# Projections written feature-major in 512-wide matmuls, transposes by DMA, weight gradients in 288 to 432 wide tiles

## The chip, the cores and the metric

One core of a Trainium2 chip runs the whole program, forward and backward. The metric is the device time of one execution in microseconds. The kernel before takes 5262.92 us (median of 3 runs, 5261.9 to 5267.33).

## The reference

The layer mixes two branches for one sequence of S = 2048 tokens of D = 576 features, and the kernel returns its output and all gradients for a given grad_out:

```
q, k, v = split(x @ wqkv)                    # H = 32 heads of 18
p = softmax(q k^T * 18^-0.5);  a = (p v) @ wo
b = fft_convolution(u, K(A, B, C, dt)) + u * Dskip   # S4, N = 128 states, u = x
g = sigmoid(sum(x * gate_w))
out = g * a + (1 - g) * b
gradients of x, wqkv, wo, A, B, C, log_dt, Dskip, gate_w
```

## The kernel before

The program has four stages, one behind the other. Tensors go between them through DRAM, and each has its own SBUF and PSUM pools, so that a stage can only load what fits after the pools of the stage before are given up. Within stage 1, post and S4 a scheduler orders each engine's instructions; in attention the order on PE, ACT, DVE and POOL is written out by hand, and the scheduler orders only the DMA queue. Every DMA here, transposes too, is issued by SP, in order, with at most eight outstanding.

**Stage 1 (lines 96 to 248).** x is loaded token-major and turned into xT (features on partitions) by 80 PE transposes of 128 x 128, each with a copy out of PSUM by DVE or ACT (lines 117 to 121); wo likewise by 25 (line 129). Then for K, Q and V in turn, for each of 16 token tiles and each of 11 chunks of 3 heads (54 columns), five matmuls accumulate over the 576 features (`ps_proj`, two PSUM buffers), and ACT (line 168) or DVE (line 170) copies the chunk into `Xa`, in which each head has 32 columns (18 and padding), with column 18 as an additional row for the softmax shift: 1 for K and V, and for Q minus the product of the norms, from squares, sums and the largest key norm (lines 178 to 187). `Xa` is stored token-major (line 191) and turned by 384 PE transposes (line 198) with copies (lines 200 and 202) into feature-major tiles of 4 heads x 32 rows, 2048 tokens wide, stored per group of heads as `QaT_d`, `KaT_d`, `VaT_d` (line 204). The gate is one more column of the last V chunk. Then grad_out times the gate (`d_a`, line 223) is transposed by 80 PE transposes, and dO = d_a wo^T is made in 960 matmuls of 48 columns (line 241) and stored at once at the end (line 248).

**Attention (lines 260 to 533).** Eight groups of four heads, four blocks of 512 queries each, forward and backward interleaved by hand. `load_group` loads a group's QaT, KaT, VaT (line 282) and the token-major Vtok, Ktok, Qtok (line 285); Ktok and Qtok have one buffer. A step makes scores twice (19 rows of contraction, 512 wide), takes two exponentials on ACT (lines 510 and 514), multiplies into `ds` on DVE (line 519), and each `ds` tile is transposed by a DMA (line 525); `accO`, `accV`, `accQ` and `accK` collect the products.

**Post (lines 536 to 678).** A first pool: O is loaded, transposed by 80 PE transposes, multiplied by wo in 960 matmuls of 48 columns (`ps_a`), reduced against grad_out for the gate's gradient (lines 577 and 578), stored times the gate; and wo's gradient in 960 matmuls of 48 (`ps_dwo`). A second pool: x and the gradient of qkv (`dqkv`) are loaded (lines 616 and 618), wqkv's gradient is made in 2880 matmuls of 48 columns, sixteen token tiles accumulated in each (`ps_dwq`), wqkv and dqkv are transposed on PE (70 and 224), and dx is made in 2688 matmuls of 48 (`ps_dx`) and stored.

**S4 (from line 702)** computes the convolution branch, its gradients and the outputs.

Of the kernel before, what the change touches and what calls it, by code (L numbers as in the profile page):

```python
# [9 lines left out]
A = mybir.AluOpType  # L10
ACT = mybir.ActivationFunctionType
BF = mybir.dt.bfloat16
# [5 lines left out]
P = 128  # L18


def build(tc, aps, dbg_aps=None, stages=("s1", "attn", "post", "s4", "final")):
# [39 lines left out]
    with ExitStack() as gctx:  # L61
# [19 lines left out]
        Qtok_d = dram.tile([P, NT * H * HP], BF, name="Qtok_d")  # L81
        Ktok_d = dram.tile([P, NT * H * HP], BF, name="Ktok_d")
        Vtok_d = dram.tile([P, NT * H * HP], BF, name="Vtok_d")
# [5 lines left out]

        with ExitStack() as ctx:  # L90
            s1 = ctx.enter_context(tc.tile_pool(name="s1", bufs=1))
            work = ctx.enter_context(tc.tile_pool(name="s1work", bufs=2))
            psA = ctx.enter_context(tc.tile_pool(name="s1psA", bufs=2, space=bass.MemoryType.PSUM))
            psB = ctx.enter_context(tc.tile_pool(name="s1psB", bufs=2, space=bass.MemoryType.PSUM))

            x_tok = s1.tile([P, NT, D], BF, name="x_tok")
            nc.sync.dma_start(x_tok, x2.rearrange("(t p) d -> p t d", p=P))
            wqkv_sb = s1.tile([P, DC, F + 1], BF, name="wqkv_sb")
            gate_w2 = gate_w.rearrange("(d o) -> d o", o=1)
            for c, (d0, dsz) in enumerate(dch):  # L100
                if dsz < P:
                    nc.gpsimd.memset(wqkv_sb[dsz:P, c, :], 0.0)
                nc.sync.dma_start(wqkv_sb[0:dsz, c, 0:F], wqkv[d0:d0 + dsz, :])
                nc.sync.dma_start(wqkv_sb[0:dsz, c, F:F + 1], gate_w2[d0:d0 + dsz, :])
            wo_sb = s1.tile([P, DC, D], BF, name="wo_sb")
            for c, (f0, fsz) in enumerate(dch):
                if fsz < P:
                    nc.gpsimd.memset(wo_sb[fsz:P, c, :], 0.0)
                nc.sync.dma_start(wo_sb[0:fsz, c, :], wo[f0:f0 + fsz, :])
            xT = s1.tile([P, DC, S], BF, name="xT")  # L110
            cnt = 0
            for c, (d0, dsz) in enumerate(dch):
                if dsz < P:
                    nc.vector.memset(xT[dsz:P, c, :], 0.0)
                for t in range(NT):
                    pt = psB.tile([P, P], BF, tag="tp", name="pt_x")
                    nc.tensor.transpose(pt[0:dsz, :], x_tok[:, t, d0:d0 + dsz], ident_bf)
                    if cnt % 2 == 0:
                        nc.vector.tensor_copy(xT[0:dsz, c, t * P:(t + 1) * P], pt[0:dsz, :])
                    else:  # L120
                        nc.scalar.copy(xT[0:dsz, c, t * P:(t + 1) * P], pt[0:dsz, :])
                    cnt += 1
            woT_sb = s1.tile([P, DC, D], BF, name="woT_sb")
            for c, (e0, esz) in enumerate(dch):
                if esz < P:
                    nc.vector.memset(woT_sb[esz:P, c, :], 0.0)
                for fc_, (f0, fsz) in enumerate(dch):
                    pt = psB.tile([P, P], BF, tag="tp", name="pt_w")
                    nc.tensor.transpose(pt[0:esz, 0:fsz], wo_sb[0:fsz, fc_, e0:e0 + esz], ident_bf[0:fsz, 0:fsz])
                    if cnt % 2 == 0:  # L130
                        nc.vector.tensor_copy(woT_sb[0:esz, c, f0:f0 + fsz], pt[0:esz, 0:fsz])
                    else:
                        nc.scalar.copy(woT_sb[0:esz, c, f0:f0 + fsz], pt[0:esz, 0:fsz])
                    cnt += 1

            sg = s1.tile([P, NT], F32, name="sg")
            qsq = s1.tile([P, NT, H], F32, name="qsq")
            kmx2 = s1.tile([P, H], F32, name="kmx2")
            mt = s1.tile([P, NT, H], F32, name="mt")
            hchunks = []  # L140
            h0 = 0
            while h0 < H:
                nh = min(3, H - h0)
                hchunks.append((h0, nh))
                h0 += nh
            MAXW = 3 * DH + 1
            cnt = 0
            for which in (1, 0, 2):
                Xa = s1.tile([P, NT, H, HP], BF, tag="Xa", name="Xa")
                (nc.gpsimd if which != 0 else nc.vector).memset(Xa, 0.0)  # L150
                if which != 0:
                    nc.vector.memset(Xa[:, :, :, DH], 1.0)
                scl = c_scale if which == 0 else 1.0
                for t in range(NT):
                    for hi, (h0, nh) in enumerate(hchunks):
                        f0 = which * D + h0 * DH
                        fsz = nh * DH
                        last = (which == 2 and hi == len(hchunks) - 1)
                        if last:
                            fsz += 1  # L160
                        ps = psA.tile([P, MAXW], F32, tag="proj", name="ps_proj")
                        for c, (d0, dsz) in enumerate(dch):
                            mm(ps[:, 0:fsz], lhsT=xT[:, c, t * P:(t + 1) * P], rhs=wqkv_sb[:, c, f0:f0 + fsz],
                               start=(c == 0), stop=(c == DC - 1))
# [1102 lines left out]
```

## Time and profile before

| | us |
|---|---|
| median of 3 runs | 5262.92 (5261.9 to 5267.33) |
| the profiled execution | 5259.65 |
| its span | 5257.9 |
| PE busy in the span | 3442.0 (65%) |
| DVE busy | 3203.6 (61%) |
| ACT busy | 3065.4 (58%) |
| POOL busy | 551.4 (10%) |

The span runs from the first to the last recorded instruction. In the views below a group's row has the line, the engine, the operation, output <- input, partitions x elements and the number of instructions; behind the bar stand their busy time, the mean of one in ns, and the idle time of the engine just before them with what ended most of it. A window's row has busy time and count for each engine, then the granted TensorE clock (1.00 is full), the DMA engines' busy share and GB/s. A timeline's row has its start, its duration, and the idle time before it in brackets.

### The profile page before, as it was taken

What the parts mean: (1) busy time and instruction counts of PE and PEld (TensorE: products, weight loads), DVE (VectorE), ACT (ScalarE), POOL (GpSimd) and SP (SyncE); (2) the same over time, 40 slices, a digit from 0 to 9 for tenths busy, and PEclk for the clock granted to TensorE, in tenths of its full rate; (3) what the DMA queues carried; (4) which work ended last, traced back from release to release, by engine and by line L of the source; (5) the groups of instructions that cost most, each with busy time, mean ns of one, the idle gap of its engine ahead of it and who ended that gap; (6) DMA issues with size and microseconds to landing.
All of it is one profiled execution on the core that took longest, in us unless ns stands there. A gap on an engine that the chain in (4) does not pass through costs nothing. (4 is left out here: it accounts for less than half of the span.)

```text
span 5257.9 us, 87333 instructions
## 1 busy us (share of the span) xinstructions
PE 3442.0 (65%) x34473; PEld 1477.7 (28%) x34473; DVE 3203.6 (61%) x6274; ACT 3065.4 (58%) x6102; POOL 551.4 (10%) x750
## 2 busy tenths in 40 slices
PE   7678999999999999999999698022222222222221
PEld 5453222222222222222222586011112222211210
DVE  4433777777777777767777433200176677776668
ACT  4336998989898998989896323000053343444321
POOL 1000000000000000000000000300023333333330
PEclk8555555555555555555555788555555555555555
DMA  2123667776767767776767401322345445444436
GB/s 97 73 77 81 122 122 137 124 133 124 136 120 131 128 123 134 125 134 120 126 122 137 162 25 59 98 65 58 97 116 122 114 110 124 101 113 122 120 89 167
DMA packets 1683053, 589.85 MB, mean 112 GB/s; under 512 B 1606222, under 2 KB 1654544, under 8 KB 1672658
## 3 DMA queue, kind: packets, MB, share of 16 engines
q1 hardware_dynamic: 1682642, 584.27, 52.6%
q8 instruction: 270, 4.42, 0.3%
q14 instruction: 141, 1.16, 0.1%
HBM read 205.89 MB, written 72.07 MB: 53 GB/s over the span
## 5 line engine op out<-in xcount | busy, mean ns | idle before, releaser
L519 DVE TENSOR_TENSOR ds<-ps_P,PT 128x512 bf16<-128x512 f32 x2048 | 1328.6, 686 | 470.1 <-PE ps_P L30 262.0
L510 ACT ACTIVATE PT<-ps_P 128x512 bf16<-128x512 f32 x2048 | 1226.5, 603 | 154.5 <-PE ps_P L30 102.6
L514 ACT ACTIVATE eb<-ps_P 128x512 bf16<-128x512 f32 x2048 | 1236.0, 605 | 19.8 <-PE ps_P L30 19.3
L30 PE MATMUL ps_P<-dOaT,VaT_g 19*128 19x512 bf16 x2048 | 1197.4, 601 | 29.6 <-DMA VaT_g<-VaT_d 28.5
L30 PE MATMUL ps_P<-KaT_g,QaT_g 19*128 19x512 bf16 x2048 | 1164.7, 593 | 7.6 <-ACT PT L510 7.6
L30 PE MATMUL ps_P<-QaT_g,KaT_g 19*128 19x512 bf16 x2048 | 1053.9, 615 | 14.8 <-DMA KaT_g<-KaT_d 12.3
L30 PE MATMUL uvr<-RX,E1e 128*128 128x64 bf16 x576 | 72.4, 290 | 648.3 <-DVE E1e L932 648.3
L30 PE MATMUL accO<-PT,Vtok_g 128*32 128x512 bf16 x2048 | 331.1, 631 | 1.1 <-DMA Vtok_g<-Vtok_d 1.1
L30 PEld LDWEIGHTS <-KaT_g 19*128 19x128 bf16 x2048 | 135.7, 103 | 694.9 <-issue 669.0
L30 PEld LDWEIGHTS <-E1e 128*128 128x128 bf16 x1152 | 119.7, 123 | 724.8 <-DVE E1e L932 629.8
L30 PEld LDWEIGHTS <-VaT_g 19*128 19x128 bf16 x2048 | 197.4, 98 | 437.0 <-issue 404.8
L30 PE MATMUL accK<-dsT,Qtok_g 128*32 128x256 bf16 x4096 | 314.7, 406 | 1.8 <-DVE dqa L396 1.0
L878 ACT COPY mst<-psM 128x512 f32<-128x512 f32 x36 | 21.9, 609 | 441.1 <-PE psM L30 368.8
L30 PE MATMUL accQ<-ds,Ktok_g 128*32 128x512 bf16 x2048 | 266.9, 620 | 1.2 <-DVE dvacc L379 1.2
L30 PE MATMUL accV<-eb,dOa 128*32 128x512 bf16 x2048 | 266.9, 620 | 0.6 <-DVE dkacc L420 0.6
L546 POOL MEMSET wo_sb<- 64x576 bf16 x1 | 0.6, 573 | 2429.9 <-DMA dqkv_d<-dtk 2429.9
L865 DVE TENSOR_SCALAR xs<-xs,msk 128x3072 bf16<-128x3072 bf16 x21 | 21.4, 1020 | 379.1 <-DMA xs<-in_A_x_dram 379.1
L30 PE MATMUL psM<-xs,gyp 128*32 128x128 bf16 x576 | 54.7, 550 | 263.2 <-DMA xs<-in_A_x_dram 133.8
L30 PE MATMUL ybp<-Rw,E1n 128*128 128x31 bf16 x1152 | 71.4, 233 | 225.7 <-POOL Rw L1013 220.4
L924 ACT ACT_TABLE_LOAD x35 | 44.9, 1283 | 291.8 <-DMA abuf<-ath_d 291.6
L30 PE MATMUL ps_proj<-wqkv_sb,xT 128*128 128x54 bf16 (+2 forms) x2640 | 171.9, 218 | 43.0 <-ACT Xa L168 31.0
L30 PEld LDWEIGHTS <-QaT_g 19*128 19x128 bf16 x2048 | 178.8, 100 | 51.3 <-issue 27.6
(332 smaller groups left out, 5525.1 us busy)
## 6 DMA issues: line engine op xcount, KB each, us to landing
abuf<-ath_d SPq DMA_DIRECT2D x36, 1024.0 KB
thb<-ath_d SPq DMA_DIRECT2D x36, 1024.0 KB
T0w<-Kp_d SPq DMA_DIRECT2D x36, 512.0 KB
dsT<-ds SPq DMA_TRANSPOSE x512
dqkv_d<-dtk SPq DMA_DIRECT2D x96, 72.0 KB
dqkv_tok<-dqkv_d SPq DMA_DIRECT2D x1, 6912.0 KB
Md_d<-mst SPq DMA_DIRECT2D x144, 36.0 KB
x_tok<-in_A_x_dram SPq DMA_DIRECT2D x2, 2304.0 KB
```

Of the source, the lines that this page charges most:

```text
L30: return nc.tensor.matmul(out, lhsT=lhsT, rhs=rhs, start=start, stop=stop, **kw)
L510: nc.scalar.activation(U["PT"][i][:, j, :], ps, ACT.Exp)
L514: nc.scalar.activation(e, ps, ACT.Exp)
L519: nc.vector.tensor_tensor(U["ds"][i][:, j, :], ps, U["PT"][i][:, j, :], op=A.mult)
L546: nc.gpsimd.memset(wo_sb[fsz:P, c, :], 0.0)
L865: nc.vector.tensor_scalar(xs[:, dl, :, :], xs[:, dl, :, :], msk[:, dl:dl + 1], None, op0=A.mult)
L878: nc.scalar.copy(mst[:, :, 0:P], psM)
L924: nc.scalar.activation(abuf, abuf, ACT.Exp, scale=l0col)
```

## The change

Stage 1 loads x with its feature dimension padded to 640 and makes xT by four DMA transposes. wqkv is copied into `Wp`, where each head's 18 columns are padded with zeros to 32, so that a matmul with 128 columns of `Wp` as weights and 512 tokens of xT as the moving operand writes four heads feature-major into PSUM, in the layout that the old transposes made: 480 matmuls of 512, three PSUM buffers. The eviction adds the constant row (`onec`) or scales; for K and Q a square, and a matmul with a 0/1 matrix `hsel` that sums each head's squares into its row 18, give the norms. Tiles are ordered by group of heads, and K, Q, V within it. wo and d_a are transposed by DMA too, and dO is made in 160 matmuls of 288 with one PSUM buffer of two banks, stored per token tile.

On PE the new order in stage 1 around the end of a group's Q (`ps_proj_778` is the last Q tile, `sq_785` and `ps2_787` its squares and their sums, `ps_proj_794` and `801` are V):

```order
L30 MATMUL ps_proj_794<-xT_97,Wp_124 128x512
L30 LDWEIGHTS hsel_137
L30 MATMUL ps2_773<-sq_771,hsel_137 128x512
L30 LDWEIGHTS Wp_124
L30 MATMUL ps_proj_794<-xT_97,Wp_124 128x512
L30 LDWEIGHTS Wp_124
L30 MATMUL ps_proj_794<-xT_97,Wp_124 128x512
L30 LDWEIGHTS hsel_137
L30 MATMUL ps2_787<-sq_785,hsel_137 128x512
L30 LDWEIGHTS Wp_124
L30 MATMUL ps_proj_794<-xT_97,Wp_124 128x512
```

A head-sum matmul stands four to seven projections behind the last one of its own tile, and PE takes its instructions in this order. Before, PE ran five projections of a chunk and then the next chunk's.

In attention, `load_group` makes Vtok, Ktok and Qtok by DMA transposes from the feature-major stores; the token-major stores are gone. On SP at the end of a group, before:

```order
L282 DMA QaT_g<-QaT_d 128x2048
L282 DMA VaT_g<-VaT_d 128x2048
L525 DMA_TRANSPOSE dsT<-ds 128x16x128
L282 DMA KaT_g<-KaT_d 128x2048
L341 DMA dqkv_d<-dtk 128x4x72
L285 DMA Ktok_g<-Ktok_d 128x16x128
L525 DMA_TRANSPOSE dsT<-ds 128x16x128
L341 DMA dqkv_d<-dtk 128x4x72
```

and now:

```order
L241 DMA QaT_g<-QaT_d 128x2048
L241 DMA VaT_g<-VaT_d 128x2048
L484 DMA_TRANSPOSE dsT<-ds 128x16x128
L241 DMA KaT_g<-KaT_d 128x2048
L300 DMA dqkv_d<-dtk 128x4x72
L244 DMA_TRANSPOSE Ktok_g<-KaT_d 128x16x128
L484 DMA_TRANSPOSE dsT<-ds 128x16x128
L300 DMA dqkv_d<-dtk 128x4x72
```

The places in the queue are the same; the plain loads have become transposes. On ACT and DVE the order in attention is the same.

Post has one pool. All its inputs are issued at once, wqkv's gradient comes first (320 matmuls of 432 columns, sixteen token tiles accumulated in each), then the output projection (160 of 288, O transposed by four DMA transposes, the gate's gradient by one fused instruction per tile), dx (448 of 288, dqkv transposed by sixteen DMA transposes, three buffers), and most of wo's gradient (160 of 288) last. On SP behind attention, now:

```order
L500 DMA O_tok<-O_d 128x16x576
L503 DMA wo_sb_37550<-in_A_wo_dram 128x576 x4
L503 DMA wo_sb_37550<-in_A_wo_dram 64x576
L505 DMA x_tok_b<-in_A_x_dram 128x16x576
L508 DMA dqkv_tok<-dqkv_d 128x16x1728
L512 DMA wq_pad<-in_A_wqkv_dram 128x1728 x4
L512 DMA wq_pad<-in_A_wqkv_dram 64x1728
L515 DMA_TRANSPOSE wqkvT<-wq_pad 128x14x128 x5
L537 DMA_TRANSPOSE OT_37945<-O_tok 128x20x128
```

Before, x and dqkv stood behind all of the output projection's stores. In S4 only a row sum is merged from 12 matmuls into 2.

The diff, cut to its core (of what is removed, the section on the kernel before tells):

```diff
@@ stage 1: start, weights, gate, d_a
-            psA = ctx.enter_context(tc.tile_pool(name="s1psA", bufs=2, space=bass.MemoryType.PSUM))
+            psA = ctx.enter_context(tc.tile_pool(name="s1psA", bufs=3, space=bass.MemoryType.PSUM))
...
+            for tb in range(NBK):
+                nc.sync.dma_start(x_pad[:, tb * TB:(tb + 1) * TB, 0:D], x_v0[:, tb * TB:(tb + 1) * TB, :])
             for c, (d0, dsz) in enumerate(dch):
+                nc.sync.dma_start(wqkv_sb[0:dsz, c, :], wqkv[d0:d0 + dsz, :])
+                nc.sync.dma_start(gw_sb[0:dsz, c:c + 1], gate_w2[d0:d0 + dsz, :])
+            for tb in range(NBK):
+                nc.sync.dma_start_transpose(out=xT[:, tb * TB:(tb + 1) * TB, :, :].rearrange("p t c q -> p (t c) q"),
+                                            in_=x_pad[:, tb * TB:(tb + 1) * TB, :].rearrange("p t d -> p (t d)"))
...
+            Wp = s1.tile([P, DC, W3, HP], BF, name="Wp")
             for c, (d0, dsz) in enumerate(dch):
+                (nc.gpsimd if c % 2 else nc.vector).memset(Wp[:, c, :, DH:HP], 0.0)
+                wv = wqkv_sb[0:dsz, c, :].rearrange("p (a d) -> p a d", d=DH)
+                if c % 2 == 0:
+                    nc.vector.tensor_copy(Wp[0:dsz, c, :, 0:DH], wv)
+                else:
+                    nc.scalar.copy(Wp[0:dsz, c, :, 0:DH], wv)
...
+            for c in range(DC):
+                nc.sync.dma_start_transpose(out=woT[:, :, c * P:(c + 1) * P], in_=wo_pad[:, c, :])
+            d_aT = s1.tile([P, NT, DC, P], BF, name="d_aT")
+            for tb in range(NBK):
+                nc.sync.dma_start_transpose(out=d_aT[:, tb * TB:(tb + 1) * TB, :, :].rearrange("p t c q -> p (t c) q"),
+                                            in_=d_a[:, tb * TB:(tb + 1) * TB, :].rearrange("p t d -> p (t d)"))
+
@@ stage 1: projections and dO
+            for g in range(NG):
+                for which in (1, 0, 2):
+                    stg = work.tile([P, S], BF, tag="stg", bufs=3, name="stg")
+                    for tb in range(NBK):
+                        ps = psA.tile([P, TB, P], F32, tag="proj", name="ps_proj")
+                        for c, (d0, dsz) in enumerate(dch):
+                            mm(ps, lhsT=Wp[0:dsz, c, which * H + 4 * g:which * H + 4 * (g + 1), :].rearrange("p a b -> p (a b)"),
+                               rhs=xT[0:dsz, tb * TB:(tb + 1) * TB, c, :], start=(c == 0), stop=(c == DC - 1))
+                        psf = ps.rearrange("p t q -> p (t q)")
+                        dst = stg[:, tb * TB * P:(tb + 1) * TB * P]
+                        if which == 0:
+                            nc.scalar.mul(dst, psf, c_scale)
+                        elif which == 1 or tb % 2 == 0:
+                            nc.scalar.add(dst, psf, onec)
+                        else:
+                            nc.vector.tensor_scalar(dst, psf, onec, None, op0=A.add)
+                        if which == 2:
+                            continue
+                        sq = work.tile([P, TB * P], BF, tag="sq", bufs=3, name="sq")
+                        nc.vector.tensor_tensor(sq, dst, dst, op=A.mult)
+                        ps2 = psB.tile([P, TB * P], F32, tag="ps2", name="ps2")
+                        mm(ps2, lhsT=hsel, rhs=sq)
+                        if which == 1:
+                            nc.vector.tensor_reduce(kmx[:, g, tb:tb + 1], ps2, axis=AX.X, op=A.max)
+                        else:
+                            sh = work.tile([P, TB * P], BF, tag="sh", bufs=3, name="sh")
+                            nc.scalar.activation(sh, ps2, ACT.Sqrt, scale=kmxg[:, g:g + 1])
+                            nc.vector.tensor_tensor(dst, dst, sh, op=A.subtract)
+                    if which == 1:
+                        nc.vector.tensor_reduce(kmxg[:, g:g + 1], kmx[:, g, :], axis=AX.X, op=A.max)
+                    nc.sync.dma_start([QaT_d, KaT_d, VaT_d][which][g], stg)
...
+            for t in range(NT):
+                psd = psB.tile([P, 2, 512], F32, tag="dO", bufs=1, name="ps_dO")
+                for u, (f0, fsz) in enumerate(HALF):
                     for c, (e0, esz) in enumerate(dch):
+                        mm(psd[:, u, 0:fsz], lhsT=d_aT[0:esz, t, c, :], rhs=woT[0:esz, c, f0:f0 + fsz],
                            start=(c == 0), stop=(c == DC - 1))
+                dO_t = work.tile([P, D], BF, tag="dO_t", bufs=3, name="dO_t")
+                if t % 2 == 0:
+                    nc.vector.tensor_copy(dO_t.rearrange("p (u f) -> p u f", u=2), psd[:, :, 0:DH2])
+                else:
+                    nc.scalar.copy(dO_t.rearrange("p (u f) -> p u f", u=2), psd[:, :, 0:DH2])
+                nc.sync.dma_start(dO_d[:, t, :], dO_t)
@@ attention: load_group
-                    for nm, src, nb in (("Vtok", Vtok_v, 2), ("Ktok", Ktok_v, 1), ("Qtok", Qtok_v, 1)):
+                    for nm, src, nb in (("Vtok", VaT_d[g], 2), ("Ktok", KaT_d[g], 1), ("Qtok", QaT_d[g], 1)):
                         T[nm] = ga.tile([P, NT, 4, HP], BF, tag=nm, bufs=nb, name=nm + "_g")
-                        nc.sync.dma_start(T[nm], src[:, :, 4 * g:4 * g + 4, :])
+                        nc.sync.dma_start_transpose(out=T[nm].rearrange("p t h w -> p t (h w)"), in_=src)
@@ post
+                O_tok = pb.tile([P, NT, DPAD], BF, name="O_tok")
+                nc.sync.dma_start(O_tok[:, :, 0:D], O_d)
+                wo_sb = pb.tile([P, DC, D], BF, name="wo_sb2")
                 for c, (f0, fsz) in enumerate(dch):
                     nc.sync.dma_start(wo_sb[0:fsz, c, :], wo[f0:f0 + fsz, :])
+                x_tok = pb.tile([P, NT, D], BF, name="x_tok_b")
+                nc.sync.dma_start(x_tok, x_v)
+                dqkv_tok = pb.tile([P, NT, FPAD], BF, name="dqkv_tok")
+                nc.sync.dma_start(dqkv_tok[:, :, 0:F], dqkv_d)
+                wq_pad = pb.tile([P, DC, FPAD], BF, name="wq_pad")
+                for c, (d0, dsz) in enumerate(dch):
+                    nc.sync.dma_start(wq_pad[0:dsz, c, 0:F], wqkv[d0:d0 + dsz, :])
+                wqkvT = pb.tile([P, FC, DPAD], BF, name="wqkvT")
+                for c in range(DC):
+                    nc.sync.dma_start_transpose(out=wqkvT[:, :, c * P:(c + 1) * P], in_=wq_pad[:, c, :])
+
+                gi = 0
+                for c, (d0, dsz) in enumerate(dch):
+                    ob = work.tile([P, F], BF, tag="dwq_bf", name="dwq_bf")
+                    for u in range(4):
+                        ps = pps.tile([P, FQ], F32, tag="pdwq", name="ps_dwq")
+                        for t in range(NT):
+                            mm(ps[0:dsz, :], lhsT=x_tok[:, t, d0:d0 + dsz], rhs=dqkv_tok[:, t, u * FQ:(u + 1) * FQ],
+                               start=(t == 0), stop=(t == NT - 1))
+                        if gi % 2 == 0:
+                            nc.scalar.copy(ob[0:dsz, u * FQ:(u + 1) * FQ], ps[0:dsz, :])
+                        else:
+                            nc.vector.tensor_copy(ob[0:dsz, u * FQ:(u + 1) * FQ], ps[0:dsz, :])
+                        gi += 1
+                    nc.sync.dma_start(out_dwqkv[d0:d0 + dsz, :], ob[0:dsz, :])
...
+                    if t % TB == 0:
+                        OT4 = work.tile([P, TB, DC, P], BF, tag="OT4", name="OT4")
+                        nc.sync.dma_start_transpose(out=OT4.rearrange("p t c q -> p (t c) q"),
+                                                    in_=O_tok[:, t:t + TB, :].rearrange("p t d -> p (t d)"))
+                    go_t = work.tile([P, D], BF, tag="go_t2", bufs=3, name="go_t2")
+                    nc.sync.dma_start(go_t, go_v[:, t, :])
+                    nc.vector.tensor_scalar(d_a_tok[:, t, :], go_t, g_t[:, t:t + 1], None, op0=A.mult)
+                    ps = pps.tile([P, 2, 512], F32, tag="ps2b", name="ps_a")
+                    for u, (e0, esz) in enumerate(HALF):
+                        for c, (f0, fsz) in enumerate(dch):
+                            mm(ps[:, u, 0:esz], lhsT=OT4[0:fsz, t % TB, c, :], rhs=wo_sb[0:fsz, c, e0:e0 + esz],
+                               start=(c == 0), stop=(c == DC - 1))
+                    ga_st = work.tile([P, D], F32, tag="ga_st", name="ga_st")
+                    nc.scalar.mul(ga_st.rearrange("p (u f) -> p u f", u=2), ps[:, :, 0:DH2], g_t[:, t:t + 1])
+                    nc.sync.dma_start(ga_d[:, t, :], ga_st)
+                    prod = work.tile([P, D], F32, tag="prod_a", bufs=1, name="prod_a")
+                    nc.vector.scalar_tensor_tensor(prod.rearrange("p (u f) -> p u f", u=2), ps[:, :, 0:DH2], 1.0,
+                                                   go_t.rearrange("p (u f) -> p u f", u=2), op0=A.mult, op1=A.mult,
+                                                   accum_out=ago[:, t:t + 1])
...
+                    dqT = work.tile([P, FC, P], BF, tag="dqT", bufs=3, name="dqT")
+                    nc.sync.dma_start_transpose(out=dqT, in_=dqkv_tok[:, t, :])
+                    ps = pps.tile([P, 2, 512], F32, tag="ps2b", name="ps_dx")
+                    for u, (e0, esz) in enumerate(HALF):
+                        for fc_, (f0, fsz) in enumerate(fch):
+                            mm(ps[:, u, 0:esz], lhsT=dqT[0:fsz, fc_, :], rhs=wqkvT[0:fsz, fc_, e0:e0 + esz],
+                               start=(fc_ == 0), stop=(fc_ == FC - 1))
+                    dxm = work.tile([P, D], F32, tag="dxm", name="dxm")
+                    if t % 2 == 0:
+                        nc.vector.tensor_copy(dxm.rearrange("p (u f) -> p u f", u=2), ps[:, :, 0:DH2])
+                    else:
+                        nc.scalar.copy(dxm.rearrange("p (u f) -> p u f", u=2), ps[:, :, 0:DH2])
+                    nc.sync.dma_start(dxm_d[:, t, :], dxm)
...
```

361 lines of the change are left out of this document (70 added, 291 removed).

## The prediction

> **What bounds the kernel now.** I cut the span into its stages first: how busy each engine is, and at which TensorE clock.
>
> ```profile
> core 0: us, PE busy (x) PEld busy (x) DVE busy (x) ACT busy (x) POOL busy (x), PEclk, DMA share, GB/s
> 0.00:460.00 460.00, 322.76 (x4173) 236.46 (x4174) 175.98 (x720) 170.77 (x682) 32.55 (x16) 0.64 0.22 80
> 460.00:2886.00 2426.00, 2380.76 (x17020) 626.57 (x17015) 1797.69 (x3007) 2181.24 (x4255) 0.00 (x0) 0.50 0.71 126
> 2886.00:3266.00 380.00, 310.24 (x7872) 267.85 (x7868) 137.95 (x566) 117.66 (x517) 13.80 (x22) 0.85 0.23 80
> 3266.00:5258.00 1992.00, 428.25 (x5416) 346.85 (x5416) 1091.96 (x1981) 595.78 (x648) 505.00 (x712) 0.53 0.44 108
> ```
>
> The rows are stage 1 (projections, dO), attention, the stage behind it ("post": weight gradients, dx) and S4. The change can shorten the first and the third, 840 us together; in S4 it only merges a few matmuls (12 into 2), which I cost at nothing.
>
> Attention is bound by ACT. Two groups of the page:
>
> ```profile
> L510 ACT ACTIVATE PT<-ps_P 128x512 bf16<-128x512 f32 x2048 | 1226.5, 603 | 154.5 <-PE ps_P L30 102.6
> L514 ACT ACTIVATE eb<-ps_P 128x512 bf16<-128x512 f32 x2048 | 1236.0, 605 | 19.8 <-PE ps_P L30 19.3
> ```
>
> 4096 exponentials at 0.60 us, pipelined, cover ACT's 2181 of 2426 us. The change alters no exponential, so only the loads at the head boundaries can move this stage.
>
> Stage 1 by groups (first 620 us):
>
> ```profile
> L30 PE MATMUL ps_proj<-wqkv_sb,xT 128*128 128x54 bf16 (+2 forms) x2640 | 171.9, 218 | 43.0 <-ACT Xa L168 31.0 <-DVE Xa L170 3.1
> L198 PE MATMUL pt_tp<-ident_bf,Xa 128*128 128x128 bf16 x384 | 82.2, 274 | 55.7 <-ACT stg L202 41.4 <-ACT Xa L187 5.1 <-DVE stg L200 4.4
> L30 PE MATMUL ps_dO<-woT_sb,d_aT 128*128 128x48 bf16 x960 | 54.5, 206 | 5.3 <-ACT dO_tok L246 0.3
> ```
>
> Five short matmuls, an eviction, five more: PE waits for evictions, and each matmul is only 36 to 54 columns. What remains is start, transposes and their evictions.
>
> **Which clock.** The forecast needs the price of 512 columns at both clocks, and which clock will be granted. Windows of 10 us and more:
>
> ```profile
> 90.00:100.00 10.00, 8.78 (x143) 7.43 (x142) 4.83 (x20) 4.71 (x20) 0.00 (x0) 1.00 0.08 31
> 120.00:130.00 10.00, 6.20 (x33) 3.33 (x32) 3.66 (x17) 4.36 (x17) 0.00 (x0) 0.50 0.26 109
> 170.00:180.00 10.00, 8.68 (x143) 7.20 (x141) 4.33 (x17) 4.50 (x17) 0.00 (x0) 0.50 0.01 2
> 2950.00:2960.00 10.00, 9.70 (x297) 8.96 (x295) 6.28 (x24) 4.68 (x22) 0.00 (x0) 1.00 0.24 84
> 3020.00:3100.00 80.00, 77.53 (x2694) 76.02 (x2692) 21.81 (x92) 17.45 (x88) 0.00 (x0) 0.98 0.10 34
> ```
>
> The projections run 143 matmuls in 10 us at granted clock 1.00 (90 us) and at 0.50 (170 us) alike: the clock does not set their pace, the round of eviction and buffer does. The transposes between (120 us) come with 0.50, and the short projection groups do not bring 1.00 back. In post, where the 16-step accumulations of dWqkv (3020 us) keep PE fed, it is 0.97 to 1.00 and 48 columns cost 80/2694 = 29.7 ns.
>
> A full-width price, from attention at 0.50:
>
> ```profile
> 2605.05 1.04 PE L30 MATMUL accQ<-ds,Ktok_g 128*32 128x512 bf16 x8
> 2607.23 0.61 PE L30 MATMUL accK<-dsT,Qtok_g 128*32 128x256 bf16 x8
> ```
>
> Eight matmuls fill 32 columns of the array each, so four run side by side: two rounds of 512 take 1.04 us, two of 256 take 0.61. The 512 additional columns cost 0.43 us at clock 0.50. I take half, 0.215, at 1.00 (288 wide 0.121, 432 wide 0.181); the other bound is post's 29.7 ns per 48 columns, 0.317 per 512.
>
> In the new order a projection tile at clock 0.50 is 5 x 0.43 = 2.15 us against an eviction of 0.61 and three buffers, so PE is always fed there. That is the state in which post got 1.00; I take 1.00.
>
> [...]
>
> **Stage 1, new.** Removed: 2640 projections, 384+80+80+25 PE transposes with evictions, 960 dO matmuls. Added: 480 projections of 512, 64 head sums of 512, 160 dO matmuls of 288, 13 DMA transposes.
>
> Start. Loads and a DMA transpose as the trace shows them (the transpose window lies behind one E1n issue in S4):
>
> ```profile
> 0.00:20.00 20.00, 6.25 (x36) 3.50 (x37) 5.71 (x19) 5.27 (x16) 16.89 (x11) 1.00 0.85 266
> 4200.00:4202.00 2.00, 0.17 (x2) 0.00 (x0) 1.01 (x4) 0.59 (x1) 0.00 (x0) 0.97 1.16 216
> L525 SPq DMA_TRANSPOSE dsT<-ds x512: 1315/1871/4891, 506.1 to 2877.8; - x171
> ```
>
> x and wqkv (4.35 MB) at 266 GB/s 16.4 us; four xT transposes of 0.66 MB at 216 GB/s 3.0 us each, 12.1: first projection at about 22, all of xT at about 28.
>
> Body, per group of four heads: PE (60 + 8) x 0.215 = 14.6 us. ACT 14 x 0.605 = 8.5. DVE by
>
> ```profile
> L1051 DVE TENSOR_TENSOR rr<-pB 128x480 bf16<-128x480 bf16 x18 | 7.6, 421 | 0.0
> L519 DVE TENSOR_TENSOR ds<-ps_P,PT 128x512 bf16<-128x512 f32 x2048 | 1328.6, 686 | 470.1 <-PE ps_P L30 262.0
> ```
>
> 8 squares and 4 subtractions at 0.43, 4 maxima and 2 evictions from PSUM at 0.69: 9.3. PE bounds. But PE runs in order, and a tile's head sum waits for its eviction (0.61) and square (0.43), some 1.4 us with handoffs; by the order it stands 4 to 7 projections later, 0.9 to 1.5 us. Where four stand between (about three places in a group) about 0.5 us is exposed: 1.5 us, so 16.2. Eight groups 130. One-offs (head-padded weights; d_a on DVE; the first Q store behind four d_aT transposes on SP) 9; 3 us of the first group lie in the start. 28 + 130 + 9 - 3 = 164.
>
> dO: one PSUM buffer, so a tile is 10 x 0.121 = 1.21 plus an eviction of 576 columns by
>
> ```profile
> L577 DVE TENSOR_TENSOR prod_a<-a_st,go_tok 128x576 f32<-128x576 f32 x16 | 12.1, 758 | 1.6
> 447.80 0.33 SPq L248 DMA_DIRECT2D dO_d<-dO_tok  x1
> 455.10 0.42 SPq L282 DMA_DIRECT2D KaT_g<-KaT_d  x1
> 459.85 0.61 PE L30 MATMUL ps_P<-QaT_g,KaT_g 19*128 19x512 bf16 x4 [12.32 <-DMA KaT_g<-KaT_d]
> ```
>
> 0.76 and 0.2 of handoff: 2.2 us, times 14.5 tiles behind the projections 32 us; 196. Then the last store and KaT's load: 4.75 us for the load as now, 2.75 for a store of 147 KB instead of 7.3: 203. Now it is 459.85: **gain 257**. Bounds: no exposure and no one-offs, 182 (gain 278); 0.317 per 512 columns, 203 + 544 x 0.102 + 14.5 x 10 x 0.058 = 267 (gain 193).
>
> **Attention, new.** Token-major V, K, Q come by DMA transposes from the feature-major stores; every other instruction stands in the old order. Ktok and Qtok have one buffer, so they load at a group's end:
>
> ```profile
> 2606.14 0.55 SPq L285 DMA_DIRECT2D Ktok_g<-Ktok_d  x1
> 2615.67 1.04 PE L30 MATMUL accQ<-ds,Ktok_g 128*32 128x512 bf16 x8
> 2620.61 0.55 SPq L285 DMA_DIRECT2D Qtok_g<-Qtok_d  x1
> 2627.38 0.61 PE L30 MATMUL accK<-dsT,Qtok_g 128*32 128x256 bf16 x8
> ```
>
> 9.5 and 6.8 us from issue to use. A transpose of 512 KB needs 2.4 us at 216 GB/s, plus an issue of 1.3 to 4.9 us on SP (the dsT row), behind which that queue's ds transposes wait. Most fits; I charge 0.6 us at each of 7 boundaries, 4 us (bounds 0 and 10 each, 70: rival C).
>
> **Post, new.**
>
> ```profile
> 2886.21 0.45 SPq L542 DMA_DIRECT2D O_tok<-O_d  x1
> 2992.36 1.93 SPq L618 DMA_DIRECT2D dqkv_tok<-dqkv_d  x1
> 3017.43 2.76 PE L30 MATMUL ps_dwq<-dqkv_tok,x_tok_b 128*128 128x48 bf16 x65 [28.54 <-DMA dqkv_tok<-dqkv_d]
> L30 PE MATMUL ps_dx<-wqkvT,dqT 128*128 128x48 bf16 x2688 | 106.1, 192 | 8.3 <-ACT dxm L676 3.6 <-ACT dqT L665 2.6
> 3264.79 0.60 PE L30 MATMUL psr<-x_t,J_bf 128*128 128x288 bf16 x2 [2.40 <-DMA x_t<-in_A_x_dram]
> ```
>
> Today x and dqkv (9.44 MB) are issued only behind the output projection and PE waits 28.5 us. Now O, wo, x and dqkv (12.4 MB) are issued together; at 9.44 MB in 25 us that is 33, plus 2 of latency, 35. Then dWqkv first: 320 x 0.181 = 58, plus 1.5 of filling. Output projection: 16 tiles, 10 x 0.121 of PE against 0.76 to 1.1 of ACT and DVE on two buffers, 1.6 us each with the waits for OT's transposes, 26, and 6 for 31 interleaved dWo matmuls and the first go loads: 32. dx: 448 x 0.121 = 54 and 1 of filling; its dqT transposes (0.46 MB, 2.1 us) hide under 3.4 us of PE per tile, three buffers. dWo's other 129: 16. The x_t load for S4 2.5. Sum 35 + 59.5 + 32 + 55 + 16 + 2.5 = 200 for 380: **gain 180**. Bounds: 0.178 per 288 and 0.267 per 432 columns (the 48-column price) cost 320 x 0.086 + 737 x 0.057 = 70 (gain 110); no filling or waits, 15 less (gain 195).
>
> **Sum.** 257 + 180 - 4 = 433. The profiled execution took 5259.65 us, 1.75 around its span of 5257.9; the median of the runs is 3.3 above it. 5257.9 - 433 = 4825 of span, 4827 profiled, **4830** as a median.
>
> **Rivals.**
>
> A. Stage 1 stays at 0.50 or swings between the clocks. For it: attention lies at 0.50 throughout although PE counts as busy for 2381 of 2426 us, and the old projections at 170 us did not come back to 1.00. Against: these have micro-waits or narrow tiles, which the new groups lack. Price: 544 x 0.215 = 117 for the body less the 12 of exposure, which slower matmuls cover, plus 14.5 x 10 x 0.121 = 17 for dO: up to 121. 4890 to 4951.
>
> B. The round trip eviction, square, head sum is exposed at nearly every tile. For it: the old projections' 43.0 us of idle stand mostly behind ACT's eviction; against: three buffers and 4 to 7 matmuls between. Some 1 us at each of 64 sums less the 12 counted: 4880 to 4895.
>
> C. The transposed loads are late at the boundaries: issue at the long end (4.9) and ds transposes behind it, 10 us x 7: 4896.
>
> D. Slower than before. The transposes from DRAM fall into 2-byte pieces. The queue's row:
>
> ```profile
> q1 hardware_dynamic: 1682642, 584.27, 52.6%
> ```
>
> is 52.6% x 16 x 5257.9 us / 1682642 = 26.3 ns per packet; 262,144 pieces of 2 bytes for 512 KB over 16 engines would be 431 us, 24 times. It decides from 433/24 = 18 us additional per transpose; with the slack of 7 to 10 us at the boundaries, from about 25. Against: the transposes out of SBUF move at 216 GB/s. If true, far over 5263.
>
> **Chances.** Forecast 0.60, A 0.17, B 0.10, C 0.09, D 0.03, no effect (the gain goes elsewhere) 0.01. The likeliest gives 4830. The range: down to 4770 (gains of 278 and 195 make 4790; 20 more for a start whose transposes overlap the loads), up to 4960, which takes in A, B and C and, but for 4 us, both bounds of the matmul price (193 + 110 - 4 = 299: 4964). A difference counts from 0.2% (10 us): faster 0.96 (all but D and no effect), same 0.01, slower 0.03.
>
> **What would show it.** Stage 1: granted clock near 1.00 from 40 to 160 us, and the first attention matmul near 203; at 0.50 it is A. Idle of PE ahead of the head-sum matmuls: 12 us in all, 60 for B. Waits of accQ and accK for Ktok and Qtok: near none, for C about 70. The first dWqkv matmul 35 us behind attention's end; the distance from attention's end to S4's first matmul near 200. S4 unchanged at 1992. I am wrong if attention's length moves by over 20 us either way, or if post's matmuls are dearer than half of attention's column price.

## The result

The changed kernel takes 4872.71 us (median of 4 runs, 4872.27 to 4874.1) beside 5263.74 for the kernel before: a ratio of 0.9257, interval 0.9241 to 0.9273. A second series gave 4870.84 and again 0.9257 (0.9243 to 0.927). 4830 was forecast, within 4770 to 4960; the gain is 391 us where 433 were summed. By stretches of the profiled execution, in us:

| stretch | before | forecast | after |
|---|---|---|---|
| to attention's first matmul | 459.9 | 203 | 230.4 |
| attention, to the issue of O's load | 2426.3 | 2430 | 2429.2 |
| post, to S4's first matmul | 378.6 | 200 | 213.6 |
| S4 | 1993.1 | 1992 | 1999.2 |
| span | 5257.9 | 4825 | 4872.4 |

The 47 us too many stand in stage 1 (27), post (14) and S4 (7), less 1 in attention. The windows of the changed kernel by stage (a row: busy us and count per engine, granted TensorE clock, DMA share, GB/s):

```profile
0.00:230.00 230.00, 192.28 (x784) 67.51 (x784) 87.86 (x186) 83.10 (x125) 10.29 (x29) 0.90 0.46 130
230.00:2655.00 2425.00, 2381.57 (x17008) 626.69 (x17012) 1798.37 (x3007) 2182.22 (x4255) 0.49 (x2) 0.50 0.72 127
2655.00:2873.00 218.00, 171.76 (x1108) 103.62 (x1104) 32.74 (x77) 24.86 (x41) 9.57 (x6) 0.90 0.72 191
2873.00:4872.00 1999.00, 428.68 (x5408) 346.48 (x5408) 1092.41 (x1982) 593.59 (x647) 507.76 (x712) 0.53 0.44 108
```

PE's records in stage 1 fall from 4173 to 784 and in post from 7872 to 1108; attention and S4 show the same busy times as before. Inside stage 1, projections (100 us) and dO (180 us and later):

```profile
100.00:110.00 10.00, 10.00 (x41) 3.20 (x40) 4.23 (x8) 4.82 (x8) 0.00 (x0) 1.00 0.26 105
180.00:190.00 10.00, 7.64 (x34) 3.44 (x34) 0.76 (x1) 1.28 (x2) 0.00 (x0) 0.72 0.17 59
200.00:210.00 10.00, 7.84 (x28) 3.04 (x27) 0.76 (x1) 1.13 (x2) 0.00 (x0) 0.50 0.13 45
```

The projections run at full clock, as forecast, but at 41 matmuls in 10 us, 0.244 us each, not 0.215. In dO the clock falls to 0.50 (first record of it at 184.4 us). These two are what the experiments take apart first. The timeline of the projections shows where 0.244 comes from, on PE and on its weight loads:

```profile
108.46 1.67 PE L30 MATMUL ps_proj<-xT,Wp 128*128 128x512 bf16 x6
109.96 0.38 PE L30 MATMUL ps<-sq,hsel 128*128 128x512 bf16 x1
...
102.54 0.09 PEld L30 LDWEIGHTS <-Wp 64*128 64x128 bf16 x1 [0.42 <-issue]
102.86 0.55 PEld L30 LDWEIGHTS <-Wp 128*128 128x128 bf16 x4 [0.23 <-issue]
103.83 0.09 PEld L30 LDWEIGHTS <-Wp 64*128 64x128 bf16 x1 [0.42 <-issue]
```

Six projections and the start of the next matmul are 1.50 us, six times 0.215 and 0.21 more. 576 features are four chunks of 128 and one of 64. The weights of the 64-row chunk, and those of the 128-row chunk behind it, are loaded only when their matmul's turn has come, 4 ns ahead of it (102.539 for 102.543 us, 102.858 for 102.862; between equal rows it is 0.21 us, 103.090 for 103.304): the weight loads stand idle for 0.42 and 0.23 us just before them.

### The profile page after: what moved, and what is told of

The parts are those of the page before. It is cut to its first block, busy times and chain, and to the rows that moved or that the text cites. A ratio compares the mean times of both kernels' runs of the same rounds, so it can differ in the third digit from the quotient of the medians.

```text
span 4872.4 us, 64871 instructions
## 1 busy us (share of the span) xinstructions
PE 3174.3 (65%) x24304; PEld 1144.3 (23%) x24304; DVE 3011.4 (62%) x5252; ACT 2883.8 (59%) x5068; POOL 528.1 (11%) x747
## 5 line engine op out<-in xcount | busy, mean ns | idle before, releaser
L355 DVE TENSOR_TENSOR dqa<-dqa,accQ 128x512 f32<-128x512 f32 x224 | 153.8, 687 | 48.9 <-PE accQ L30 48.6
```

The costliest lines, as they stand in the source:

```text
L355: nc.vector.tensor_tensor(U["dqa"], U["dqa"], acc, op=A.add)
```

## The experiments

All start from the changed kernel (4871 to 4873 us, spans of 4872.4 and 4873.1). "First attention matmul" is the end of stage 1, 230.4 and 232.3 us in its two profiled executions.

**128 rows everywhere.**

```diff
+                if dsz < P:
+                    nc.vector.memset(Wp[dsz:P, c, :, 0:DH], 0.0)
...
-                            mm(ps, lhsT=Wp[0:dsz, c, which * H + 4 * g:which * H + 4 * (g + 1), :].rearrange("p a b -> p (a b)"),
-                               rhs=xT[0:dsz, tb * TB:(tb + 1) * TB, c, :], start=(c == 0), stop=(c == DC - 1))
+                            mm(ps, lhsT=Wp[:, c, which * H + 4 * g:which * H + 4 * (g + 1), :].rearrange("p a b -> p (a b)"),
+                               rhs=xT[:, tb * TB:(tb + 1) * TB, c, :], start=(c == 0), stop=(c == DC - 1))
...
-                        mm(psd[:, u, 0:fsz], lhsT=d_aT[0:esz, t, c, :], rhs=woT[0:esz, c, f0:f0 + fsz],
+                        mm(psd[:, u, 0:fsz], lhsT=d_aT[:, t, c, :], rhs=woT[:, c, f0:f0 + fsz],
...
```

> The fifth chunk of every contraction uses all 128 rows (its padding is zero in both operands) instead of 64: projections, dO, output projection and dx; nothing else changes. In the changed kernel 128-row matmuls of 512 follow each other at 0.215 us, but a 64-row one starts 0.31 us after its forerunner and the next 128-row one 0.32 us after it. Theory (a switch of the row count costs about 0.1 us each way): a projection tile falls from 1.29 to 1.08 us, 96 tiles give 20 us, dO (at clock 0.50) some 8, so that the first attention matmul stands at about 202 instead of 230; dx and the output projection give 6 each; span 4832. Rival (the end of a tile costs it, by the change of the PSUM bank and the semaphore of the last matmul): the fifth matmul keeps its 0.31, span 4872.

4824.44 us (4821.4 to 4831.29), ratio 0.9171 (0.9158 to 0.9185). First attention matmul 195.6. The last projection starts at 157.8 instead of 174.8, 17.0 us earlier; its timeline:

```profile
103.30 1.46 PE L30 MATMUL ps_proj<-xT,Wp 128*128 128x512 bf16 x6
104.59 0.38 PE L30 MATMUL ps<-sq,hsel 128*128 128x512 bf16 x1
```

1.29 us for six: the 0.21 is gone, though a tile still ends with the same semaphore and change of bank. Post shortens by 6 (207.6), dx from 61.6 to 55.0; the 6 that were expected of the output projection did not come (35.9 for 34.9). The first attention matmul gains 35 and not 28: dO now keeps its clock,

```profile
160.00:190.00 30.00, 18.91 (x138) 13.12 (x135) 5.30 (x7) 4.25 (x7) 0.00 (x0) 1.00 0.24 85
```

which was not expected, with the one buffer and its waits still there. The row switch stands; what takes the clock was open again.

**Every second tile in reverse order**, so that two 64-row chunks meet.

```diff
+                        order = list(enumerate(dch))
+                        if tb % 2 == 1:
+                            order = order[::-1]
-                        for c, (d0, dsz) in enumerate(dch):
+                        for k, (c, (d0, dsz)) in enumerate(order):
...
-                               rhs=xT[0:dsz, tb * TB:(tb + 1) * TB, c, :], start=(c == 0), stop=(c == DC - 1))
+                               rhs=xT[0:dsz, tb * TB:(tb + 1) * TB, c, :], start=(k == 0), stop=(k == DC - 1))
```

> Every second projection tile takes its five chunks in the reverse order, so that the 64-row chunk that ends a tile stands next to the 64-row chunk that begins the next. Theory (the price is the switch between 128 and 64 rows, 0.10 us each way): a V tile falls from 1.29 to about 1.18 us, the first attention matmul moves from 230 to 222 to 226. Rival (the 64-row matmul itself is dearer by 0.2): 1.29 and 230.

4857.78 us (4854.6 to 4863.01), ratio 0.9228 (0.9213 to 0.9243). The last projection starts at 166.2, 8.6 us earlier, half of the 17.0 for half of the switches. The first attention matmul, at 225.0, gains only 5.4, in the main since the clock fell 4.4 us into dO here (at 170.8) and 9.2 us into it in the changed kernel. Weight loads:

```profile
104.39 0.11 PEld L30 LDWEIGHTS <-Wp 64*128 64x128 bf16 x2 [0.42 <-issue]
104.93 0.10 PEld L30 LDWEIGHTS <-Wp 128*128 128x128 bf16 x1 [0.42 <-issue]
```

The two 64-row loads come together; the idle time stands before the first of them and behind the second. The price is the switch, not the 64-row matmul. In the changed kernel's trace each change of the row count costs 0.10 us: a 64-row matmul starts 0.312 us after the 128-row one ahead of it (102.543 after 102.231 us), the next 128-row one 0.319 us after that, and between equal rows it is 0.215. Why a change costs this is not shown by a run.

**dO through three one-bank buffers**, a half at a time.

```diff
-                psd = psB.tile([P, 2, 512], F32, tag="dO", bufs=1, name="ps_dO")
+                    psd = psA.tile([P, TB, P], F32, tag="proj", name="ps_dO").rearrange("p t q -> p (t q)")
...
+                    if u == 0:
+                        nc.vector.tensor_copy(dO_t[:, f0:f0 + fsz], psd[:, 0:fsz])
+                    else:
+                        nc.scalar.copy(dO_t[:, f0:f0 + fsz], psd[:, 0:fsz])
```

> dO's halves of 288 columns go through the three one-bank PSUM buffers of the projections, each half evicted alone, instead of one two-bank buffer per token tile. Theory (PE's waits for the single buffer, about 1 us in each tile, let the clock fall to 0.50 at 184 us): the clock stays at 1.00 through dO, a half costs 5 x 0.12 + 0.2, the dO stretch falls from 47 to about 26 us, span 4851. Rival (the clock falls for another reason, the width of 288 or the time spent at full clock): 0.50 from about 184 us as before, only the evictions hidden, some 9 us, span 4863.

4845.02 us (4842.74 to 4848.74), ratio 0.9211 (0.9196 to 0.9226). First attention matmul 206.2; dO runs from 174.0 to 200.0 us, 26 us as expected, at full clock:

```profile
175.00:199.00 24.00, 24.00 (x149) 11.76 (x147) 6.75 (x15) 5.83 (x15) 0.00 (x0) 1.00 0.30 107
```

So the width of 288 does not take it away. The time spent at full clock does not either, though that is shown by the other run: with 128 rows it lasted 157 us (35.6 to 192.6), in the changed kernel 143, here 140 (63.6 to 203.5). Taking away the waits keeps it, and taking away the switches did too.

**One buffer for the projections.**

```diff
-            psA = ctx.enter_context(tc.tile_pool(name="s1psA", bufs=3, space=bass.MemoryType.PSUM))
+            psA = ctx.enter_context(tc.tile_pool(name="s1psA", bufs=1, space=bass.MemoryType.PSUM))
```

> The projections get one PSUM buffer instead of three, so that PE waits for an eviction (about 0.95 us) after each tile. Theory (short waits after every tile take the clock away): granted clock 0.50 in the projections, a tile costs 5 x 0.43 + 0.24 + 0.95 = 3.3 us, 96 tiles 320 us, first attention matmul near 425, span near 5065. Rival (waits of 1 us don't touch the clock): 1.29 + 0.95 = 2.24 us per tile, 215 us, first attention matmul near 321, span near 4965.

4909.3 us (one run), first attention matmul 273.4: both expectations missed. PE waited 0.7 to 0.8 us behind every tile's eviction, and still the clock held until 222 us:

```profile
140.00:210.00 70.00, 46.44 (x176) 16.63 (x175) 24.85 (x49) 22.74 (x35) 0.00 (x0) 1.00 0.15 60
225.00:260.00 35.00, 27.44 (x58) 7.30 (x58) 8.87 (x19) 8.57 (x13) 0.00 (x0) 0.50 0.11 45
```

The theory that short waits as such take the clock falls: the same waits stood there at full clock since 130 us. The total is low since the scheduler put all dO tiles into the waits (55 to 130 us). A better reading is the share of time in which columns stream: 176 matmuls of 0.215 us in 70 us are 0.54. This mean is of two kinds of tile: K and Q with their head sums, 6 x 0.215 in 2.27 to 2.36 us or 0.55 to 0.57, and V, 10 x 0.215 in the 4.31 us of two tiles or 0.50. The clock was lost among V tiles, and V tiles just like them had kept it in the group before:

```profile
195.21 1.34 PE L30 MATMUL ps_proj<-xT,Wp 128*128 128x512 bf16 x5 [0.78 <-ACT stg L181]
197.40 1.34 PE L30 MATMUL ps_proj<-xT,Wp 128*128 128x512 bf16 x5 [0.84 <-DVE stg L183]
...
220.24 1.34 PE L30 MATMUL ps_proj<-xT,Wp 128*128 128x512 bf16 x5 [0.84 <-DVE stg L183]
222.36 2.40 PE L30 MATMUL ps_proj<-xT,Wp 128*128 128x512 bf16 x5 [0.78 <-ACT stg L181]
```

In the changed kernel's dO the share is less:

```profile
176.77 1.70 PE L30 MATMUL ps_dO<-woT,d_aT 128*128 128x288 bf16 x10 [0.73 <-ACT dO_t L211]
179.31 1.70 PE L30 MATMUL ps_dO<-woT,d_aT 128*128 128x288 bf16 x10 [0.85 <-DVE dO_t L209]
181.74 1.70 PE L30 MATMUL ps_dO<-woT,d_aT 128*128 128x288 bf16 x10 [0.73 <-ACT dO_t L211]
```

Two tiles take 4.97 us, of which 20 x 0.12 stream: 0.48, and the clock fell. With 128 rows everywhere it was 138 x 0.12 in the 30 us of that run's row: 0.55, and it held, with waits of the same length:

```profile
163.86 1.39 PE L30 MATMUL ps_dO<-woT,d_aT 128*128 128x288 bf16 x10 [0.73 <-ACT dO_t L213]
166.15 1.39 PE L30 MATMUL ps_dO<-woT,d_aT 128*128 128x288 bf16 x10 [0.90 <-DVE dO_t L211]
```

So the length of the waits alone does not decide it.

**Each dO tile copied out twice**, on top of 128 rows everywhere: no switch, longer waits.

```diff
                     nc.vector.tensor_copy(dO_t.rearrange("p (u f) -> p u f", u=2), psd[:, :, 0:DH2])
+                    nc.vector.tensor_copy(dO_t.rearrange("p (u f) -> p u f", u=2), psd[:, :, 0:DH2])
...
                     nc.scalar.copy(dO_t.rearrange("p (u f) -> p u f", u=2), psd[:, :, 0:DH2])
+                    nc.scalar.copy(dO_t.rearrange("p (u f) -> p u f", u=2), psd[:, :, 0:DH2])
```

> 128 rows everywhere, one dO buffer, and each dO tile copied out twice (the second copy rewrites the first), so that PE waits some 1.7 us for the buffer instead of 0.95. No switch of the row count is left. Theory (the clock goes by the share of time in which the array is fed: it fell at 0.46, held at 0.53 to 0.55): 1.2 of 2.9 us is 0.41, the clock falls to 0.50 some 8 us into the stretch of dO tiles. Rival (the row switches took the clock): it stays at 1.00 to the end of dO.

4845.68 us (one run), first attention matmul 218.9. The clock falls at 171.1 us, 13 us into the dO tiles:

```profile
166.41 1.39 PE L30 MATMUL ps_dO<-woT,d_aT 128*128 128x288 bf16 x10 [1.40 <-ACT dO_t L215]
169.49 1.40 PE L30 MATMUL ps_dO<-woT,d_aT 128*128 128x288 bf16 x10 [1.70 <-DVE dO_t L212]
172.29 2.56 PE L30 MATMUL ps_dO<-woT,d_aT 128*128 128x288 bf16 x10 [1.40 <-ACT dO_t L215]
```

The same ten matmuls take 1.40 us and then 2.56. Two tiles in 5.88 us are 0.41. Switches are not needed for the fall. A border near 0.5 in the share, an estimate from these runs alone (fallen at 0.41 and 0.48, held at 0.55), fits all these cases, but not the time to the fall: 13 us at 0.41, and at 0.48, in the four executions with the changed kernel's dO, 9.2, 4.1 (its repetition below), 6.6 (x and dqkv first) and 4.4 us (every second tile in reverse).

**x and dqkv loaded first in post.**

```diff
+                x_tok = pb.tile([P, NT, D], BF, name="x_tok_b")
+                nc.sync.dma_start(x_tok, x_v)
+                dqkv_tok = pb.tile([P, NT, FPAD], BF, name="dqkv_tok")
+                nc.gpsimd.memset(dqkv_tok[:, :, F:FPAD], 0.0)
+                nc.sync.dma_start(dqkv_tok[:, :, 0:F], dqkv_d)
                 O_tok = pb.tile([P, NT, DPAD], BF, name="O_tok")
```

> Behind attention x and dqkv are loaded ahead of O and wo. Theory (the first weight gradient matmul waits for all bytes issued up to dqkv, 12.4 MB at 385 GB/s): 3.0 MB less ahead of it, it starts 8 us earlier, span 4865. Rival (its wait is for issue and latency, or the O transposes come later by the same 8 us and give it back): span 4872.

4855.87 us (4852.57 to 4860.53), ratio 0.923 (0.9214 to 0.9244). From the first load of post to the first gradient matmul 26.1 us instead of 36.7, to S4's first matmul 202.6 instead of 213.6: 11 us. By the expectation's figures the bytes are worth 8; no run separates them from the order on SP. That wo's five loads held SP too fits the timeline of the changed kernel, where dqkv is issued only 6.4 us behind O:

```profile
2659.65 0.60 SPq L500 DMA_DIRECT2D O_tok<-O_d  x1
2660.30 5.04 SPq L503 DMA_DIRECT2D wo_sb<-in_A_wo_dram  x5
2666.01 5.53 SPq L508 DMA_DIRECT2D dqkv_tok<-dqkv_d  x1
```

Nothing was given back by O's transposes. Of the 20 us by which the span fell, another 11 are S4, which ran 1988.5 us here without any change to it.

**The changed kernel again**, as a measure.

> The changed kernel once more, as the measure for the three beside it: 4873, and what of attention (2429 us) and S4 (1999 us) moves although nothing in them differs. Theory: both stages scatter by some 5 us between profiled executions, S4 lies between 1988 and 1999. Rival (S4 is really 6 us longer after the change): 1999 again.

Attention 2429.1, S4 1994.2, post 217.5. Over all these kernels, in none of which S4 differs, S4 lies between 1988.5 and 1999.2, so the 6 us by which S4 was longer after the change are within the scatter between executions.

**The three together**: 128 rows, three buffers for dO, x and dqkv first.

> 128 rows everywhere, dO through the three one-bank buffers, x and dqkv loaded first, all together. Theory (three separate costs): the projections end at about 157 us, dO costs 32 x 0.6 at clock 1.00, first attention matmul near 182; post 207.6 - 13.5 = 194; span 4799. Rival (128 rows and three buffers take the same loss of the dO stretch): first attention matmul near 195, span 4812.

4803.19 us (4802.03 to 4806.24), ratio 0.9127 (0.9114 to 0.9141). First attention matmul 184.8 (182 expected), post 194.0 (194), span 4800.3 (4799): the theory holds. The gains in stage 1 do not simply add up (34.8 us for the rows and 24.2 for the buffers alone, 45.6 together), since each of the two alone already keeps the full clock in dO. dO runs from 159.1 to 178.6 us, 0.122 us per matmul of 288.

**dqkv in four column quarters** on top of these.

```diff
-                nc.sync.dma_start(dqkv_tok[:, :, 0:F], dqkv_d)
+                for u in range(4):
+                    nc.sync.dma_start(dqkv_tok[:, :, u * FQ:(u + 1) * FQ], dqkv_d[:, :, u * FQ:(u + 1) * FQ])
...
-                for c, (d0, dsz) in enumerate(dch):
-                    ob = work.tile([P, F], BF, tag="dwq_bf", name="dwq_bf")
-                    for u in range(4):
+                for u in range(4):
+                    for c, (d0, dsz) in enumerate(dch):
+                        ob = work.tile([P, FQ], BF, tag="dwq_bf", bufs=4, name="dwq_bf")
...
```

> As the three together, and dqkv loaded in four column quarters, with wqkv's gradient made quarter by quarter. Theory (the first gradient matmul waits for bytes): x and a quarter are 4.1 MB, it starts some 15 us behind the load of x instead of 24, span 9 us below the three together, about 4790. Rival (pieces of 864 bytes instead of 3456 load more slowly, or PE waits for a later quarter): no gain, about 4799.

4815.57 us (4814.06 to 4817.6), ratio 0.915 (0.9136 to 0.9164): 12 us slower than the three alone. The first gradient matmul does come 13.9 us behind x's load, but then PE stands:

```profile
2628.93 20.78 PE L30 MATMUL ps_dwq<-dqkv_tok,x_tok_b 128*128 128x432 bf16 x96 [16.88 <-DMA dqkv_tok<-dqkv_d]
2669.26 21.05 PE L30 MATMUL ps_dwq<-dqkv_tok,x_tok_b 128*128 128x432 bf16 x105 [19.55 <-ACT dwq_bf L531]
...
2654.01 11.94 SPq L520 DMA_TRANSPOSE wqkvT<-wq_pad  x5
2666.00 2.51 SPq L535 DMA_DIRECT2D out_dram<-dwq_bf  x4
```

The four output buffers are full, and their stores stand on SP behind five transposes. The wait named in neither expectation was the one that counted.

**The same with twelve output buffers.**

```diff
-                        ob = work.tile([P, FQ], BF, tag="dwq_bf", bufs=4, name="dwq_bf")
+                        ob = work.tile([P, FQ], BF, tag="dwq_bf", bufs=12, name="dwq_bf")
```

> As the four quarters, with twelve buffers for wqkv's gradient on its way out instead of four. With four, PE stood 19.5 us behind an eviction that had no free buffer, since the stores stand on SP behind five transposes of wqkv, which wait for the loads. Theory (that is all that the quarters lost): twelve buffers at 2.9 us each reach past the first store, no wait, behind attention's end 184 us instead of 194 with the three alone, span 4790. Rival (the smaller pieces or the later quarters are late themselves): PE waits for a dqkv quarter instead, 4800 or more.

4793.36 us (4792.13 to 4794.38), ratio 0.9111 (0.9096 to 0.9127). The 320 gradient matmuls run without a wait,

```profile
2627.25 62.05 PE L30 MATMUL ps_dwq<-dqkv_tok,x_tok_b 128*128 128x432 bf16 x320 [16.96 <-DMA dqkv_tok<-dqkv_d]
```

post takes 183.4 us, the span 4790.4, as expected. This version is the fastest: 468 us below the kernel before measured beside it, some 79 below the changed one.

## Why the prediction was right or wrong

**What bounds the kernel, and where the change could act: right.** Attention moved by 3 us (forecast 4), no more than it scatters between the executions of the changed kernels (2427.9 to 2431.5). The groups that use the transposed loads, before and then after:

```profile
L30 PE MATMUL accK<-dsT,Qtok_g 128*32 128x256 bf16 x4096 | 314.7, 406 | 1.8 <-DVE dqa L396 1.0
L30 PE MATMUL accQ<-ds,Ktok_g 128*32 128x512 bf16 x2048 | 266.9, 620 | 1.2 <-DVE dvacc L379 1.2
...
L30 PE MATMUL accK<-dsT,Qtok_g 128*32 128x256 bf16 x4096 | 315.1, 406 | 1.7 <-DVE dqa L355 0.8
L30 PE MATMUL accQ<-ds,Ktok_g 128*32 128x512 bf16 x2048 | 266.9, 620 | 1.2 <-DVE dvacc L338 1.2
```

Their idle time is what it was and stands behind DVE, not behind a load of Ktok or Qtok: neither rival C's price was paid nor D's. S4 stayed within its scatter.

**Which clock: right for the projections, on a false reading.** The prediction took the old projections' 143 matmuls in 10 us "at granted clock 1.00 (90 us) and at 0.50 (170 us) alike" as a sign that their pace was not set by the clock. The 1.00 was no measurement. In the kernel before the first record of a granted clock stands at 100.7 us, in the changed kernel at 41.0; ahead of it the column shows 1.00. The changed kernel's matmuls tell it:

```profile
37.96 2.99 PE L30 MATMUL ps_proj<-xT,Wp 128*128 128x512 bf16 x6
46.15 2.21 PE L30 MATMUL ps_proj<-xT,Wp 64*128 64x512 bf16 x8
```

Six in 2.99 us at 38 us, where the column says 1.00, eight in 2.21 at 46. And the old kernel's groups from 60 to 100 and from 160 to 200 us have one mean:

```profile
L30 PE MATMUL ps_proj<-wqkv_sb,xT 128*128 128x54 bf16 x496 | 32.4, 221 | 5.0 <-ACT Xa L168 2.3 <-DVE Xa L170 0.8
L30 PE MATMUL ps_proj<-wqkv_sb,xT 128*128 128x54 bf16 x499 | 32.4, 221 | 5.8 <-ACT Xa L168 3.0 <-DVE Xa L170 0.8
```

The other half of the argument, that at 0.50 PE is always fed in the new order and that this brings 1.00, is what happened: full clock from 41 to 184 us. Rival A did not come true for the projections (its sum, 117 - 12 + 17, is 122 and not 121). Nor did its other form, a swing between the clocks: one record of 1.00 covers the changed kernel's projections from 41.0 us to their end.

**dO: the step that failed, 17 us of stage 1's 27.** The prediction priced a tile at 2.2 us "10 x 0.121 = 1.21 plus an eviction" and kept the clock at 1.00. The 14.5 tiles behind the projections took 49 us instead of 32. At full clock a tile took 2.49 us, which makes 36: 4 of the 17 us are the row switches, and the other 13 came since the clock fell after three and a half tiles. Without the switches the price was right: with 128 rows the same tiles took 31.5 us at full clock. Rival A has 17 us for dO too, but that the two numbers agree is chance: A's are all 14.5 tiles at a clock that stays at 0.50, without the switches. What the runs put in place of the kept clock: shares of 0.48 and 0.41 lost it, 0.55 kept it, and at 0.50 both were seen.

**The price of a projection: right between equal rows, and a term was missing.** 0.215 us was met to the digit, and 0.121 per 288 nearly (0.122). The prediction counted every matmul alike and never asked about the 64-row chunk; 96 tiles x 0.21 are 20 us (17 measured by taking it away), and dx (61.6 us for 55) has it as well. The prediction's last sign of being wrong, post's matmuls dearer than half of attention's column price, is met there: 61.6 us for 448 are 0.137 each, and 0.123 with 128 rows.

**Exposed head sums: wrong, in the other direction.** 12 us were charged, and the rows quoted show none: six projections and the switch fill 1.50 us to the digit. Over all head sums from 48 us on, the step from the matmul before them is 1.8 us in sum above 0.215 each, leaving out the switches. The switches give the eviction and the square time that they need: with 128 rows the same excess is 4.9 us, and 3 of the 20 us are not gained there. So the projections ended 11 us late (175 for 164): 20 for the switches, some 4 for matmuls at half clock from 33 to 41 us (18 x 0.215), less 10 of exposure; some 3 less in the start and the one-offs were not taken apart. The errors have opposite signs, so a part of how near the total came is luck. Rival B was not paid.

**Post: right in its parts, 13.5 us over in all.** Loads 36.7 (35), gradient of wqkv 61.9 (59.5), output projection 34.9 (32), dx 61.6 (55), dWo and S4's load 18.5 (18.5). dx is the row switch, which 128 rows took away; the load term was sized rightly, but 11 us of it went when x and dqkv were loaded first.

## What to carry to other kernels

Price a matmul by its neighbours as well: here a contraction that ended in a 64-row chunk paid 0.10 us for the change of rows twice per group, and padding it with zeros, at the cost of a memset, ended the 96 tiles 17.0 us earlier. Before giving a stage to the full clock, work out the share of time in which columns stream, tile by tile with its waits; here three and a half tiles at a share of 0.48 ran at full clock, and the 11 behind them at 0.50. And where loads are brought forward on one queue, look at what stands behind them there: the stores that free buffers wait too (PE stood 19.55 us behind them in the four quarters).

## What the hardware showed beyond that

All figures of this section are measured in this case's runs or worked out from their traces. The full clock was kept at a share of 0.55 (dO with 128 rows, 31 us) and lost at 0.48 (the changed kernel's dO, 4 to 9 us into it in four executions) and at 0.41 (two copies, 13 us into it). With one buffer for the projections a mix of tiles at 0.50 and at 0.55 to 0.57 kept it for some 90 us, and then it was lost among those at 0.50. Once lost, a share of 0.71 at half clock (58 x 0.43 in 35 us, the second row of the one-buffer run) did not bring it back in 35 us, while the dense start of the projections (PE busy in 20.00 of the 20 us from 20 to 40) was followed by it at 41 us. The waits between the changed kernel's dO tiles, where it was lost, were 0.73 to 0.91 us long, with ten matmuls of 0.12 us in a tile of 2.49; waits of the same length did no harm with 128 rows, where a tile took 2.20 us (two in 4.40, from 170.55 to 174.95). Whether 0.5 is the border, and whether it is the share of columns or of something near it that counts, stays open: no finer steps were measured, and nothing here explains how long the fall took.
